# Cosine up products in one-pass pieces from the fourth chunk on, and a planner that orders from both ends

## The chip, the cores and the metric

The kernel runs on one core of a Trainium2 chip. The metric is the device time of one execution in microseconds (us). Engines are named as in the profile: PE (TensorE; PEld is its weight load), DVE (VectorE), ACT (ScalarE), POOL (GpSimd) and SP, which issues the transfers.

## The reference

A Fourier mixing of the input along the sequence and the feature axis, of which the real part is kept, then a two-layer network with a leaky ReLU between:

```python
# x: 8 x 3008 x 256, w_in: 256 x 2048, w_out: 2048 x 256, all float32
X = np.fft.fft(x, axis=1)
X = np.fft.fft(X, axis=2)
x = X.real.astype(np.float32).reshape(8 * 3008, 256)
h = x @ w_in
g = np.maximum(0.01 * h, h)
out = (g @ w_out).astype(np.float32)
```

## The kernel before, in words

**The mathematics.** The transform over features is folded into `w_in` once, at the start: `wf(0, ...)` holds the weights of the cosine part and `wf(1, ...)` those of the sine part, 128 rows by 2048 hidden columns each. The transform over the sequence (`even_rows`, `odd_rows`, `butterfly`) makes `mix_sb[0]` and `mix_sb[1]`, the cosine and sine parts of one batch element with the frequencies as columns, in units: 16 units, two for a batch element. A column of frequency k and the one of -k have the same cosine and opposite sine products, so a hidden value is cosine + sine for the one and cosine - sine for the other. One feature row that doesn't fit in 128 (the Nyquist row, `nb_sb`, with its weights `wn`) is put into the cosine bank beforehand by ScalarE: that is the *seed*.

**Chunks and steps.** The columns are cut into 23 chunks of 504 or 498 columns (`Chunk`, index `t` from 0); a batch element has three, the first only two because its first columns go through a start-up path (`HEAD`, `START`). Each chunk has 16 steps, one for each block of 128 hidden values (`f`). A step (`up`, `up_end`, `hidden`):

- ACT writes the seed into a cosine bank in PSUM (`seed`), two banks in turn for each of cosine and sine;
- PE adds the cosine product, weights `wf(0)` by `mix_sb[0]`, to the seed, and makes the sine product in a sine bank;
- ACT copies the cosine bank to SBUF, DVE writes copy + sine and copy - sine as hidden blocks (`block_sb`), ACT applies the leaky ReLU to them.

The second layer (`sum`, `product`, `combine`) multiplies the hidden blocks with `w_out` in a scheme with fewer products than the plain one: DVE and POOL form sums of blocks (`SUMS`), PE multiplies them with stored combinations of weights (26 products of four matmuls for a chunk, 104 down products, each 252 or 249 columns), and ACT and DVE combine the results (`part_sb`) and send them out. Their weights are loaded anew for every chunk into a ring of eight places (`wr`), six ahead.

**Exact parts.** A float32 matmul is done as two records on PE, a matmul whose operands are of type float32r as one. From chunk 2 on (`PARTED_FROM = 2`) the sine product is done in three float32r matmuls. Each operand is split: `high` is the value scaled by 1 - 2^-13 and rounded to float32r, `low` is what is left, and `both` combines the two. The three products high x high, low x low, both x both are summed in the bank, and between the second and the third ACT scales the bank by 1 + 1/4096. The third is issued in `up_end`. The pieces of the sine columns are made in `parts`, once for a chunk: ACT writes `high`, DVE `both`, POOL `low`, into one of two `mixed` tiles in turn (`mixed[t % 2]`). The pieces of the weights are made once, in `parted_weights`, stored in DRAM (`parted_dram`) and loaded step by step, 192 KB each, four steps ahead, into the four places where the sine weights `wf(1)` lay (`Parted`).

**The order.** After the head, nothing is issued in the order of the code. `rest` calls the helpers in the order of an event list (steps, with offsets such as `UP_FROM`, `UP_END`, `PARTS_AT`), and each call to an engine is only recorded (`Order`, `Taker`). That order fixes what depends on what: reads, writes, buffers reused. `Order.hand_on` then derives the dependences (`connect`), plays the program through with a price for each instruction (`Op.cost`, `SEEN`, and `PORT_LEFT` for instructions of DVE and POOL that may not overlap), and emits all instructions sorted by the start that this gives (`time`). When an engine is free, `time` takes the ready instruction with the earliest `latest`, a due time found by going back from PE's instructions in the order of the code. Since all are emitted from one line, every profile row reads L481.

Of the kernel before, what the change touches and what calls it, by code (L numbers as in the profile page):

```python
# [19 lines left out]
P = 128  # L20
# [121 lines left out]
PARTED_FROM = 2  # L142
UPPER, SHIFT = 1.0 - 2.0**-13, 2.0**12
PARTS_AT, PARTED_WEIGHTS_AT, UP_END = -2.7, 18, 0.2
# [193 lines left out]
SEEN = {"PE": 0.053, "ACT": 0.033, "DVE": 0.033, "POOL": 0.078, "SP": 0.05}  # L338
NAMES = {"tensor": "PE", "scalar": "ACT", "vector": "DVE", "gpsimd": "POOL", "sync": "SP"}
# [124 lines left out]
class Order:  # L464
# [11 lines left out]
    def hand_on(self):  # L476
        self.connect()
        self.time()
        for op in sorted(self.ops, key=lambda op: (op.start, op.at)):
            how = {name: viewed(a) for name, a in op.how.items()}  # L480
            op.made = getattr(op.real, op.method)(*map(viewed, op.args), **how)  # L481
            if op.gate is not None:
                self.add_gate(op.made, op.gate.made)

    def connect(self):
        places = {}
        for at, op in enumerate(self.ops):
            op.at = at
            op.busy, op.took, op.port = op.cost()
            to = op.args[0] if op.args else op.how["out"]  # L490
            reads = [a for a in (*op.args[1:], *op.how.values()) if is_ap(a)]
            name, written = stretches_of(to)
            for a in reads:
# [18 lines left out]
            op.before.discard(at)  # L512
            for b in op.before:
                self.ops[b].after.append(at)

    def time(self):
        ops, engines = self.ops, ("PE", "ACT", "DVE", "POOL", "SP")
        t = 0.0
# [6 lines left out]
        for op in reversed(ops):  # L525
            for b in op.after:
                op.latest = min(op.latest, ops[b].latest - SEEN[ops[b].engine] - op.took)
# [102 lines left out]
def tile_fnet_leaky_relu(  # L630
# [32 lines left out]
    small_sb = const.tile([P, NF + 10], F32, name="small")  # L663
    half_sb = const.tile([P, 568 + 2 * KC + 384], F32, name="half")
# [231 lines left out]
    wf_cos = const.tile([P, F], F32, name="wf_cos")  # L896
    wf_sin = [late.tile([P, WN], F32, name=f"wf_sin{i}", tag=f"wf{i}") for i in range(F // WN)]

    def wf(i, at, n):

        if i == 0:
            return wf_cos[:, at : at + n]
        return wf_sin[at // WN][:, at % WN : at % WN + n]
# [5 lines left out]
    parted_dram = dram.tile([NF, P, 3 * P], F32, name="parted_dram")  # L909
# [5 lines left out]
    angle, inf, lrelu, touched = (small_sb[:, NF + at : NF + at + n] for at, n in ((0, 6), (6, 2), (8, 1), (9, 1)))  # L915
# [205 lines left out]
    def parted_weights(f):  # L1121


# [3 lines left out]
        here = mixed[f // 2 % 2][:, 0 : 6 * P].rearrange("p (f i n) -> p f i n", f=2, i=3)  # L1127
        src = wf(1, f * P, 2 * P).rearrange("p (f n) -> p f n", f=2)
# [5 lines left out]
        nc.sync.dma_start(parted_dram[f : f + 2].rearrange("f p n -> p f n"), here.bitcast(F32).rearrange("p f i n -> p f (i n)"))  # L1134

    class Parted:


        def __init__(self):
            self.places, self.count = [], NF * (len(chunk) - PARTED_FROM)  # L1140

        def load(self, i):
            n = F // WN
            if i >= self.count:
                return
            if i < n:
                self.places.append(Late(wf_sin[i][:, 0 : 3 * P], F32R, lambda: late.tile([P, 3 * P], F32R, name=f"parted{i}", tag=f"wf{i}")))
            nc.sync.dma_start(self.places[i % n].bitcast(F32), parted_dram[i % NF])

        def weight(self, i, part):  # L1150
            return self.places[i % (F // WN)][:, part * P : (part + 1) * P]
# [421 lines left out]
    class Chunk:  # L1573
# [27 lines left out]
        def parts(self):  # L1601
# [10 lines left out]
        def product_of_parts(self, bank, at, i, start=False):  # L1612
            m = mixed[self.t % 2].rearrange("p (i n) -> p i n", i=3)
            nc.tensor.matmul(bank[:, 0 : self.w], lhsT=parted.weight(at, i), rhs=m[:, i, 0 : self.w],
                             start=start, stop=True, skip_group_check=True)

        def seed(self, f):
            nc.scalar.activation(cos_ps[self.half(f)][:, 0 : self.w], nb_sb[:, self.lo : self.lo + self.w], ACT.Copy, scale=wn[:, f : f + 1])

        def up(self, f):  # L1620
            cos, sin = cos_ps[self.half(f)], sin_ps[self.half(f)]
            in_parts = self.t >= PARTED_FROM
            if in_parts:
                at = NF * (self.t - PARTED_FROM) + f
                self.product_of_parts(sin, at, 0, start=True)
                self.product_of_parts(sin, at, 1)
                nc.scalar.activation(sin[:, 0 : self.w], sin[:, 0 : self.w], ACT.Copy, scale=1.0 + 1.0 / SHIFT)
            for i, bank in enumerate((cos, sin)[: 2 - in_parts]):
                nc.tensor.matmul(bank[:, 0 : self.w], lhsT=wf(i, f * P, P), rhs=mix_sb[i][:, self.lo : self.lo + self.w],
                                 start=(i == 1), stop=True, skip_group_check=True)  # L1630
            if not in_parts and self.t == PARTED_FROM - 1 and f % (WN // P) == WN // P - 1:
                parted.load(f // (WN // P))
# [6 lines left out]

        def up_end(self, f):  # L1640
            at = NF * (self.t - PARTED_FROM) + f
            self.product_of_parts(sin_ps[self.half(f)], at, 2)
            parted.load(at + F // WN)
# [175 lines left out]
    def rest():  # L1819
# [3 lines left out]
        parted = Parted()  # L1823
        every.extend(Chunk(t) for t in range(count))
        events = []
        for t in range(count):
            for f in range(NF):
                events.append((16 * t + UP_FROM + f, 3, t, f))
                events.append((16 * t + UP_FROM + f + (UP_END if t >= PARTED_FROM else 0.0), 5, t, f))
# [4 lines left out]
            if t >= PARTED_FROM:  # L1834
                events.append((16 * t + PARTS_AT, 4, t, 0))
# [51 lines left out]
        for _, kind, t, i in events:  # L1887
            if kind == 0:
                start_work(16 * t + i)
                if 0 <= 16 * t + i - PARTED_WEIGHTS_AT < NF // 2:  # L1890
                    parted_weights(2 * (16 * t + i - PARTED_WEIGHTS_AT))
# [18 lines left out]
            elif kind == 4:  # L1910
                every[t].parts()
            elif kind == 3:
# [3 lines left out]
                part = every[t]  # L1916
                made = part.up(i)
# [7 lines left out]
                waiting.clear()  # L1925
            else:
                part = every[t]
                if t >= PARTED_FROM:
                    part.up_end(i)
                waiting[:] = [part.hidden(*made)]  # L1930
# [247 lines left out]
```

## Time and profile before

| | |
|---|---|
| median of 3 runs | 1783.54 us (1782.3 to 1785.22) |
| profiled execution | 1785.57 us, its span 1783.8 us |
| PE, PEld busy | 1760.2, 1396.4 us |
| DVE, ACT, POOL busy | 1560.5, 1250.0, 1084.1 us |
| mean granted TensorE clock | 0.997 |
| moved by DMA | 315.26 MB, 177 GB/s on the mean |

The span is the time from the first to the last instruction in the profiled execution. Busy time is that in which an engine has at least one instruction under way; PEld overlaps PE. A row such as `sin_psa<-mixed,parted` names what is written and what is read: `cos_ps` and `sin_ps` are the banks of the up products, `sum_ps` those of the down products, `dft_ps` that of the transform, each with a letter for the bank; `mixed` holds the pieces of the columns, `parted` those of the weights, `wr` the down weights, `part` the results under combination, `block` the hidden values.

### The profile page before, as it was taken

The numbers are of one execution on the slowest core, as the hardware profiler recorded it, in microseconds if no ns is written. First come the engines' busy times: TensorE is split into PE (matmuls) and PEld (weight loads), VectorE is DVE, ScalarE is ACT, GpSimd is POOL, SyncE is SP. The second block draws the span as 40 slices with busy tenths as digits, with TensorE's granted clock in tenths as the row PEclk, the third lists the DMA queues.
The fourth block names the chain that finished last, engine by engine and source line by source line (L and its number), as shares of the span: only waits on it lengthen the run. The fifth ranks groups of instructions, "written<-read, shape, count | busy, mean of one in ns | idle before, by whom it ended". The sixth has DMA issues, their size and how long they took to land.

```text
span 1783.8 us, 24565 instructions
## 1 busy us (share of the span) xinstructions
PE 1760.2 (99%) x7568; PEld 1396.4 (78%) x7568; DVE 1560.5 (87%) x2635; ACT 1250.0 (70%) x2230; POOL 1084.1 (61%) x480
## 2 busy tenths in 40 slices
PE   9999999999999999999999999999999999999999
PEld 7867687778877888777887778877787777887788
DVE  8897888998899998898998988898989997877887
ACT  4687567876777767777677767777677786767750
POOL 2247476666766665766657657676575765576630
PEclk9999999999999999999999999999999999999999
DMA  7573456655556556555566545755557555555454
GB/s 257 165 253 137 128 159 213 202 164 172 184 182 201 157 172 207 176 187 164 169 221 190 167 148 166 245 172 165 149 172 232 170 158 153 170 150 161 146 145 140
DMA packets 194690, 315.26 MB, mean 177 GB/s; under 512 B 22896, under 2 KB 104432, under 8 KB 194560
## 3 DMA queue, kind: packets, MB, share of 16 engines
q1 hardware_dynamic: 194416, 313.69, 56.8%
q8 instruction: 61, 1.00, 0.2%
q14 instruction: 69, 0.57, 0.1%
q10 hardware_dynamic: 144, 0.00, 0.0%
HBM read 278.92 MB, written 34.68 MB: 176 GB/s over the span
## 4 chain that ended last, share of the span: by engine, by line
PE 88%; DVE 6%; DMA 2%; ACT 2%; issue 1%; SPq 0%; DVEq 0%; ACTq 0%
PE sum_psc L481 20%; PE sum_psa L481 17%; PE sum_psb L481 16%; PE cos_psb L481 8%; PE cos_psa L481 8%; PE sin_psb L481 7%; PE sin_psa L481 7%; PE dft_ps L481 3%; DVE block L481 3%; DVE xt L481 2%; DVE part L481 2%; ACT block L481 1%; DMA out_dram<-part 1%; DMA xt<-in_x_dram 1%; ACT part L481 0%
## 5 line engine op out<-in xcount | busy, mean ns | idle before, releaser
L481 POOL TENSOR_TENSOR block<-block 128x1008 f32<-128x1008 f32 (+2 forms) x402 | 1008.8, 2520 | 535.0 <-DVE block L481 298.0
L481 ACT ACTIVATE block<-block 128x504 f32<-128x504 f32 (+3 forms) x611 | 439.3, 733 | 238.2 <-DVE block L481 232.8
L481 PE MATMUL sum_psc<-block,wr 128*128 128x252 f32 (+1 forms) x1896 | 487.0, 376 | 0.0
L481 PEld LDWEIGHTS sum_psc<-block,wr 128*128 128x128 f32 x1896 | 358.5, 190 | 102.4 <-issue 64.5
L481 PE MATMUL sum_psb<-block,wr 128*128 128x252 f32 (+1 forms) x1536 | 399.5, 376 | 0.3 <-DVE part L481 0.3
L481 PE MATMUL sum_psa<-block,wr 128*128 128x252 f32 (+1 forms) x1544 | 396.9, 377 | 0.6 <-DVE wr L481 0.5
L481 DVE TENSOR_TENSOR block<-block 128x1008 f32<-128x1008 f32 (+2 forms) x249 | 362.3, 1463 | 0.3
L481 PEld LDWEIGHTS sum_psa<-block,wr 128*128 128x128 f32 x1544 | 293.0, 191 | 86.2 <-issue 54.3
L481 PEld LDWEIGHTS sum_psb<-block,wr 128*128 128x128 f32 x1536 | 286.7, 190 | 81.8 <-issue 51.8
L481 DVE TENSOR_TENSOR block<-cos,sin_psa 128x504 f32<-128x504 f32 (+1 forms) x356 | 224.8, 670 | 98.6 <-PE sin_psa L481 81.9
L481 DVE TENSOR_TENSOR block<-cos,sin_psb 128x504 f32<-128x504 f32 (+1 forms) x380 | 239.2, 670 | 47.7 <-PE sin_psb L481 42.6
L481 PE MATMUL sin_psb<-mixed,parted 128*128 128x504 f32 (+1 forms) x504 | 242.5, 524 | 13.1 <-ACT sin_psb L481 13.0
L481 DVE TENSOR_TENSOR part<-part 128x252 f32<-128x252 f32 (+1 forms) x342 | 231.3, 698 | 0.9 <-ACT part L481 0.5
L481 PE MATMUL sin_psa<-mixed,parted 128*128 128x504 f32 (+1 forms) x504 | 230.5, 511 | 0.7 <-ACT sin_psa L481 0.5
L481 PE MATMUL cos_psb<-mixc,wf_cos 128*128 128x504 f32 (+1 forms) x380 | 190.9, 584 | 0.0
L481 PE MATMUL cos_psa<-mixc,wf_cos 128*128 128x504 f32 (+2 forms) x372 | 183.1, 574 | 0.0
L481 DVE TENSOR_TENSOR xt<-xt 128x512 f32<-128x512 f32 (+5 forms) x225 | 152.7, 697 | 1.4 <-DMA xt<-in_x_dram 1.1
L481 ACT ACTIVATE cos_psb<-nb,small 128x504 f32<-128x504 f32 (+1 forms) x190 | 129.6, 682 | 4.9
L481 ACT COPY cos<-cos_psa 128x504 f32<-128x504 f32 (+1 forms) x178 | 102.6, 577 | 37.5 <-PE cos_psa L481 36.4
L481 ACT COPY cos<-cos_psb 128x504 f32<-128x504 f32 (+1 forms) x190 | 109.2, 575 | 27.6 <-PE cos_psb L481 26.0
L481 ACT ACTIVATE cos_psa<-nb,small 128x504 f32<-128x504 f32 (+2 forms) x180 | 122.4, 680 | 4.8
L481 ACT ACTIVATE sin_psa<-sin_psa 128x504 f32<-128x504 f32 (+1 forms) x168 | 96.2, 572 | 36.2 <-PE sin_psa L481 35.2
(162 smaller groups left out, 1520.5 us busy)
## 6 DMA issues: line engine op xcount, KB each, us to landing
wr<-w_dram SPq DMA_DIRECT2D x575, 256.0 KB, 2.8
parted<-parted_dram SPq DMA_DIRECT2D x336, 192.0 KB, 2.6
xt<-in_x_dram SPq DMA_DIRECT2D x28, 1024.0 KB, 6.5
out_dram<-part SPq DMA_DIRECT2D x120, 126.0 KB, 2.3
out_dram<-part SPq DMA_DIRECT2D x64, 124.5 KB, 2.2
tabe<-in_seq_tab_dram SPq DMA_DIRECT2D x29, 190.0 KB, 2.8
w_dram<-block SPq DMA_DIRECT2D x18, 256.0 KB, 4.2
block<-in_w_in_dram SPq DMA_DIRECT2D x8, 512.0 KB, 4.1
```

What stands on the lines that cost most here:

```text
L481: op.made = getattr(op.real, op.method)(*map(viewed, op.args), **how)
```

## The change

1. The cosine product is done in three float32r products too, from chunk 3 on (`PARTED_FROM = (3, 2)` for cosine and sine). Its first two are added to the seed, ACT scales the cosine bank by 1 + 1/4096 in between, and the third is added after that. So that the seed isn't scaled, it is made with `wn_less`, the Nyquist weights divided by that factor. In the list of events the two third products, and with them the copy of the cosine bank, the next seed and `hidden`, come in `up_end`, half a step later (`UP_END = 0.5`).
2. The pieces of the cosine columns are made by the same three instructions, once for a chunk. Sine and cosine have one `mixed` tile each now (`mixed[1 - part]`), not two in turn; the events that make them stand at 0.8 and 0.9 of a step into the chunk, where sine's stood at 2.7 steps ahead of it.
3. The pieces of the cosine weights are made in steps 32 to 47, one block a step, stored in `parted_dram`, and loaded like those of the sine. `wf_cos` becomes four tiles that give their places to these pieces.
4. The planner plays the program through up to 30 times (`ROUNDS`). After each round it goes through the program from the end with the starts just found (`time_back`), takes the due times from that, and plays it forward again; the shortest of the 30 orders is used. A result that PE takes from another engine counts as ready half a microsecond later than before (`SLACK = 0.5`).
5. Smaller: the angle table moves to another tile, and `parted_weights` no longer waits for a gate before its first subtraction.

The diff, cut to its core:

```diff
-PARTED_FROM = 2
+PARTED_FROM = (3, 2)
+UP_PER = 1.0
-PARTS_AT, PARTED_WEIGHTS_AT, UP_END = -2.7, 18, 0.2
+PARTS_AT, PARTED_WEIGHTS_AT, UP_END = (0.9,0.8), (32, 18), 0.5
...
+SLACK = 0.5
+ROUNDS = 30
...
     def hand_on(self):
         self.connect()
-        self.time()
+        self.place()
...
+        best = None
+        for i in range(ROUNDS):
+            if i:
+                self.time_back()
+            self.time()
+            total = max(op.start + op.took for op in ops)
+            if best is None or total < best[0]:
+                best = total, [op.start for op in ops]
+        for op, start in zip(ops, best[1]):
+            op.start = start
+
+    def time_back(self):
...
+            while soon[e] and soon[e][0][0] <= t + 1e-9:
+                k = heapq.heappop(soon[e])[1]
+                heapq.heappush(now[e], (-ops[k].start - ops[k].took, k))
...
+        for op in ops:
+            op.latest = -placed[op.at]
...
-                    ready[b] = max(ready[b], t + (SEEN[to.engine] if what == "done" else 0.0))
+                    ready[b] = max(ready[b], t + (to.seen + (SLACK if b >= self.first and to.engine == "PE" else 0.0) if what == "done" else 0.0))
...
-    wf_cos = const.tile([P, F], F32, name="wf_cos")
-    wf_sin = [late.tile([P, WN], F32, name=f"wf_sin{i}", tag=f"wf{i}") for i in range(F // WN)]
+    wfs = [[late.tile([P, WN], F32, name=f"wf_{part}{i}", tag=f"wf_{part}{i}") for i in range(F // WN)] for part in ("cos", "sin")]
...
-    def parted_weights(f):
+    def parted_weights(part, f):
...
+            nc.scalar.activation(wn_less, wn, ACT.Copy, scale=1.0 / (1.0 + 1.0 / SHIFT))
+        n = 1 + part
+        to = mixed[f // 2 % 2][:, 0 : 6 * P] if part else mixed[1][:, f % 3 * 3 * P : (f % 3 + 1) * 3 * P]
...
-        wait_for_gate(nc.gpsimd.tensor_tensor(both, src, high, op=ALU.subtract))
+        nc.gpsimd.tensor_tensor(both, src, high, op=ALU.subtract)
...
-            m = mixed[self.t % 2].rearrange("p (i n) -> p i n", i=3)
-            high, low, both = (m[:, i, 0 : self.w] for i in range(3))
-            src = mix_sb[1][:, self.lo : self.lo + self.w]
+            high, low, both = self.pieces(part)
+            src = mix_sb[part][:, self.lo : self.lo + self.w]
             nc.scalar.activation(high, src, ACT.Copy, scale=UPPER)
             nc.vector.scalar_tensor_tensor(both, in0=high, scalar=1.0 + 1.0 / SHIFT, in1=src, op0=ALU.mult, op1=ALU.subtract)
             nc.gpsimd.tensor_tensor(low, src, high, op=ALU.subtract)
...
+        def pieces(self, part):
+            m = mixed[1 - part].rearrange("p (i n) -> p i n", i=3)
+            return [m[:, i, 0 : self.w] for i in range(3)]
...
         def up(self, f):
...
+            for part, bank in reversed(list(enumerate(self.banks(f)))):
+                if self.in_parts(part):
+                    self.product_of_parts(bank, part, f, 0, start=(part == 1))
+                    self.product_of_parts(bank, part, f, 1)
+                    nc.scalar.activation(bank[:, 0 : self.w], bank[:, 0 : self.w], ACT.Copy, scale=1.0 + 1.0 / SHIFT)
+                else:
+                    nc.tensor.matmul(bank[:, 0 : self.w], lhsT=wf(part, f * P, P), rhs=mix_sb[part][:, self.lo : self.lo + self.w],
+                                     start=(part == 1), stop=True, skip_group_check=True)
...
+        def up_end(self, f):
+            cos, sin = self.banks(f)
+            for part, bank in enumerate((cos, sin)):
+                if self.in_parts(part):
+                    self.product_of_parts(bank, part, f, 2)
+                    parted[part].load(NF * (self.t - PARTED_FROM[part]) + f + F // WN)
```

More of the change, by code (lines that the diff above doesn't have):

```diff
@@ L485, in connect @@
     def connect(self):
-        places = {}
+        places, made = {}, set()
         for at, op in enumerate(self.ops):
@@ L492, in connect @@
             name, written = stretches_of(to)
+            if isinstance(to, Late) and name not in made:
+                made.add(name)
+                written = [(0, to.ap[0][0])]
             for a in reads:
@@ L512, in connect, with place @@
             op.before.discard(at)
+            op.seen = SEEN[op.engine]
             for b in op.before:
                 self.ops[b].after.append(at)
-    def time(self):
-        ops, engines = self.ops, ("PE", "ACT", "DVE", "POOL", "SP")
-        t = 0.0
+    def place(self):
+        ops, t = self.ops, 0.0
         for op in ops:
@@ new lines, in place, with at @@
+        for op, start in zip(ops, best[1]):
+            op.start = start
+    def time_back(self):
+        ops, engines = self.ops, ("PE", "ACT", "DVE", "POOL", "SP")
+        left, placed, opens = [len(op.after) for op in ops], [0.0] * len(ops), [0.0] * len(ops)
+        free, port = dict.fromkeys(engines, 0.0), {"DVE": 0.0, "POOL": 0.0}
+        soon, now, events, count = {e: [] for e in engines}, {e: [] for e in engines}, [], 0
+        def at(t, e):
+            nonlocal count
+            count += 1
+            heapq.heappush(events, (t, count, e))
+        for op in ops:
+            if not op.after:
+                heapq.heappush(soon[op.engine], (0.0, op.at))
+        for e in engines:
+            at(0.0, e)
+        while events:
+            t, _, e = heapq.heappop(events)
+            if t < free[e] - 1e-9:
+                continue
+            while soon[e] and soon[e][0][0] <= t + 1e-9:
+                k = heapq.heappop(soon[e])[1]
+                heapq.heappush(now[e], (-ops[k].start - ops[k].took, k))
+            k, waits, other = None, [], port["POOL" if e == "DVE" else "DVE"]
+            while now[e] and k is None:
+                first = heapq.heappop(now[e])
+                if ops[first[1]].port and other > t + 1e-9:
+                    waits.append(first)
+                else:
+                    k = first[1]
+            for first in waits:
+                heapq.heappush(now[e], first)
+            if k is None:
+                if waits:
+                    at(other, e)
+                elif soon[e]:
+                    at(soon[e][0][0], e)
+                continue
+            op = ops[k]
+            placed[k] = free[e] = max(t + op.busy, opens[k])
+            if op.port:
+                port[e] = placed[k]
+            for b in op.before:
+                to = ops[b]
+                opens[b] = max(opens[b], placed[k] + (to.busy if to.engine == e == "PE" else to.took + op.seen))
+                left[b] -= 1
+                if not left[b]:
+                    when = max(0.0, opens[b] - to.busy)
+                    heapq.heappush(soon[to.engine], (when, b))
+                    at(max(when, free[to.engine]), to.engine)
+            at(free[e], e)
+        for op in ops:
+            op.latest = -placed[op.at]
@@ L528, in time @@
+    def time(self):
+        ops, engines = self.ops, ("PE", "ACT", "DVE", "POOL", "SP")
         left, ready = [len(op.before) for op in ops], [0.0] * len(ops)
@@ L1146, in load, with weight @@
             if i < n:
[L1147 to L1151, printed above, removed]
+                of = ("cos", "sin")[self.part]
+                self.places.append(Late(wfs[self.part][i][:, 0 : 3 * P], F32R,
+                                        lambda: late.tile([P, 3 * P], F32R, name=f"parted_{of}{i}", tag=f"wf_{of}{i}")))
+            nc.sync.dma_start(self.places[i % n].bitcast(F32), parted_dram[self.part, i % NF])
+        def weight(self, i, piece):
+            return self.places[i % (F // WN)][:, piece * P : (piece + 1) * P]
     reach = [w % 4 for w in range(8)]
@@ L1610, in parts, with product_of_parts @@
             nc.gpsimd.tensor_tensor(low, src, high, op=ALU.subtract)
-        def product_of_parts(self, bank, at, i, start=False):
-            m = mixed[self.t % 2].rearrange("p (i n) -> p i n", i=3)
-            nc.tensor.matmul(bank[:, 0 : self.w], lhsT=parted.weight(at, i), rhs=m[:, i, 0 : self.w],
+        def pieces(self, part):
+            m = mixed[1 - part].rearrange("p (i n) -> p i n", i=3)
+            return [m[:, i, 0 : self.w] for i in range(3)]
+        def product_of_parts(self, bank, part, f, i, start=False):
+            nc.tensor.matmul(bank[:, 0 : self.w], lhsT=parted[part].weight(NF * (self.t - PARTED_FROM[part]) + f, i), rhs=self.pieces(part)[i],
@@ L1620, in up, with banks @@
+        def banks(self, f):
+            return cos_ps[self.half(f)], sin_ps[self.half(f)]
         def up(self, f):
[L1621 to L1632, printed above, removed]
+            for part, bank in reversed(list(enumerate(self.banks(f)))):
[3 more added lines that the diff above has]
+                    nc.scalar.activation(bank[:, 0 : self.w], bank[:, 0 : self.w], ACT.Copy, scale=1.0 + 1.0 / SHIFT)
+                else:
+                    nc.tensor.matmul(bank[:, 0 : self.w], lhsT=wf(part, f * P, P), rhs=mix_sb[part][:, self.lo : self.lo + self.w],
+                                     start=(part == 1), stop=True, skip_group_check=True)
@@ L1633, in up @@
+            for part in (1, 0):
+                if self.t == PARTED_FROM[part] - 1 and f % (WN // P) == WN // P - 1:
+                    parted[part].load(f // (WN // P))
+        def up_end(self, f):
[4 more added lines that the diff above has]
+                    parted[part].load(NF * (self.t - PARTED_FROM[part]) + f + F // WN)
             k, g = divmod(f, 4)
@@ L1822, in rest @@
         count = len(chunk)
-        parted = Parted()
+        parted = [Parted(part) for part in range(2)]
         every.extend(Chunk(t) for t in range(count))
@@ L1833, in rest @@
                 events.append((16 * t + (DOWN_FROM + m / PER_STEP if t else FIRST_DOWN + m / FIRST_PER), 2, t, m))
-            if t >= PARTED_FROM:
-                events.append((16 * t + PARTS_AT, 4, t, 0))
+            for part in range(2):
+                if t >= PARTED_FROM[part]:
+                    events.append((16 * t + PARTS_AT[part], 4, t, part))
         for r in range(16 * count + 18):
@@ L1889, in rest @@
                 start_work(16 * t + i)
-                if 0 <= 16 * t + i - PARTED_WEIGHTS_AT < NF // 2:
-                    parted_weights(2 * (16 * t + i - PARTED_WEIGHTS_AT))
+                for part in range(2):
+                    f = (16 * t + i - PARTED_WEIGHTS_AT[part]) * (1 + part)
+                    if 0 <= f < NF:
+                        parted_weights(part, f)
                 now[0] = START_SHARES.get(i, 0.0) if 16 * t + i < 17 else SHARES[0] if 16 * t + i < 32 else SHARES[1]
@@ L1910, in rest @@
             elif kind == 4:
-                every[t].parts()
+                every[t].parts(i)
             elif kind == 3:
@@ L1915, in rest @@
                     assert 2 * b + (hi > UW[1]) <= transformed[-1], (t, transformed, len(folds.queue))
-                part = every[t]
-                made = part.up(i)
+                every[t].up(i)
+                for to in sum(waiting, []):
+                    nc.scalar.activation(to, to, ACT.Lrelu)
+                waiting.clear()
+            else:
+                made = every[t].up_end(i)
                 seed_next(16 * t + i)
@@ L1924, in rest @@
                 behind[:] = [None]
[L1925 to L1930, printed above, removed]
+                waiting[:] = [every[t].hidden(*made)]
                 some(0)
```

41 lines of the change are left out of this document (20 added, 21 removed).

## The prediction

> **What bounds the kernel now.** I read the page's busy shares first, then PE's own waits, then the engines in six equal stretches of the steady part, then PE in order of time, then the groups by form. The shares, with two rows of the table of waits that has PE as the waiting engine:
>
> ```profile
> span 1783.8 us, 24565 instructions
> PE 1760.2 (99%) x7568; PEld 1396.4 (78%) x7568; DVE 1560.5 (87%) x2635; ACT 1250.0 (70%) x2230; POOL 1084.1 (61%) x480
> PE 88%; DVE 6%; DMA 2%; ACT 2%; issue 1%; SPq 0%; DVEq 0%; ACTq 0%
> PE sin_psb L481 <- ACT sin_psb L481: 13.0, 9, 2.8
> PE sin_psa L481 <- ACT sin_psa L481: 0.5, 1, 0.5
> ```
>
> PE is busy all the time and holds 88% of the chain that ended last. Its one repeated wait is that of a sine product for ScalarE's scaling of the same bank: 13.5 us in 10 waits. The stretches show how near the others are (columns: stretch, its length, then busy time and instructions of PE, PEld, DVE, ACT, POOL, clock, DMA share, GB/s):
>
> ```profile
> 300.00:532.00 232.00, 231.59 (x1006) 185.06 (x1005) 206.91 (x342) 171.39 (x303) 157.94 (x66) 1.00 0.59 181
> 764.00:996.00 232.00, 232.00 (x1011) 186.10 (x1010) 213.26 (x360) 175.48 (x313) 148.66 (x61) 1.00 0.60 186
> 996.00:1228.00 232.00, 230.02 (x993) 183.52 (x992) 204.17 (x354) 175.55 (x334) 153.34 (x61) 0.99 0.58 179
> sum 1392.00, PE 1378.19 PEld 1100.45 DVE 1228.15 ACT 1021.89 POOL 916.16; mean PE 229.70 PEld 183.41 DVE 204.69 ACT 170.32 POOL 152.69
> ```
>
> DVE is busy 88% on the mean (204.69 of 232) and 92% in the fullest stretch, where PE never stops. So PE sets the time and DVE is close behind it.
>
> Busy records of PE overlap, so prices come from starts, in PE's order of time in one step:
>
> ```profile
> 942.62 1.00 PE L481 MATMUL sum_psc<-block,wr 128*128 128x249 f32 x4
> 943.28 0.80 PE L481 MATMUL sin_psa<-mixed,parted 128*128 128x504 f32 x2
> 943.92 1.01 PE L481 MATMUL cos_psa<-mixc,wf_cos 128*128 128x504 f32 x2
> 944.76 1.00 PE L481 MATMUL sum_psc<-block,wr 128*128 128x249 f32 x4
> 945.42 0.58 PE L481 MATMUL sin_psa<-mixed,parted 128*128 128x504 f32 x1
> 945.83 1.42 PE L481 MATMUL sum_psc<-block,wr 128*128 128x249 f32 x6
> ```
>
> The full cosine product (two records) lasts from 943.92 to 944.76: 0.84 us. Four records of the down product take the same, 0.84 (0.21 each), so the group from 942.62 ends at 943.46, and the two sine pieces fill 943.46 to 943.92: 0.23 each. (A one-pass record begins early, when its weights are in; the next plain one marks its end.) The third: 944.76 + 0.84 = 945.60, to 945.83, 0.23 again.
>
> The groups that price the rest, and the span of one group by the tile's view (durations min/median/max, first and last start):
>
> ```profile
> L481 POOL TENSOR_TENSOR block<-block 128x1008 f32<-128x1008 f32 x270 | 681.8, 2536 | 372.5 <-DVE block L481 211.4 <-PE sum_psb L481 60.2 <-PE sum_psa L481 58.8
> L481 ACT ACTIVATE sin_psa<-sin_psa 128x504 f32<-128x504 f32 x112 | 64.3, 574 | 18.5 <-PE sin_psa L481 17.6
> L481 DVE TENSOR_TENSOR part<-part 128x252 f32<-128x252 f32 x225 | 146.2, 668 | 0.8 <-ACT part L481 0.5
> L481 DVE TENSOR_TENSOR part<-part,sum_psc 128x252 f32<-128x252 f32 x90 | 34.9, 410 | 6.4 <-PE sum_psc L481 4.9 <-ACT part L481 1.4
> L481 DVE SCALAR_TENSOR_TENSOR mixed<-mixed,mixs 128x504 fp32r<-128x504 f32 x14 | 13.2, 944 | 0.0
> L481 PE MATMUL sin_psa<-mixed,parted x504: 383/573/583, 225.9 to 1727.4; 128*128 128x504 f32 x112, 128*128 128x498 f32 x56
> L481 PEld LDWEIGHTS sin_psa<-mixed,parted x504: 186/190/198, 225.9 to 1727.4; 128*128 128x128 f32 x168
> L481 ACT ACTIVATE mixed<-mixs x21: 599/617/628, 217.5 to 1593.3; 128x504 fp32r<-128x504 f32 x14, 128x498 fp32r<-128x498 f32 x7
> L481 POOL TENSOR_TENSOR mixed<-mixs,mixed x21: 1247/1293/2220, 218.2 to 1606.0; 128x504 fp32r<-128x504 f32 x14, 128x498 fp32r<-128x498 f32 x7
> L481 DVE SCALAR_TENSOR_TENSOR mixed<-mixed,mixs x21: 664/672/2771, 221.3 to 1629.6; 128x504 fp32r<-128x504 f32 x14, 128x498 fp32r<-128x498 f32 x7
> L481 ACT ACTIVATE mixed<-wf_sin x8: 400/406/430, 89.0 to 184.5; 128x256 fp32r<-128x256 f32 x8
> L481 POOL TENSOR_TENSOR mixed<-wf_sin,mixed x8: 721/732/1756, 89.8 to 185.0; 128x256 fp32r<-128x256 f32 x8
> ```
>
> Sine in pieces runs over 21 chunks of 16 steps on two banks: 504 records a bank, three a step. From step 0 of its first chunk to step 14 of its last (20.9 chunks) there are 1501.5 us: a chunk takes 72 us.
>
> **The change part by part.** Times are set against the profiled execution (span 1783.8, with what lies around it 1785.6); the median of the runs is 1783.5, 2.1 lower.
>
> *Cosine products.* One full product becomes three one-pass ones from the fourth chunk on: 20 chunks of 16 steps, 320 times. Each saves 0.84 - 3 x 0.23 = 0.15; with the 0.23 rounded up (0.46 for a pair, and 0.22 to 0.23 alone) 0.155. That is **-50 us**, all on PE's path. Three weight loads in place of two add 320 x 0.19 = 61 us to PEld; each lies under the product before it (0.19 under 0.23), so nothing; uncovered it would cost 0.19 each.
>
> *The scaling in the cosine bank.* It is one more ScalarE instruction a step, 0.574 us, and the third product waits for it; on PE's queue the down products stand behind that product, and on ScalarE's the copy of the cosine, the next seed and the leaky ReLUs stand behind the scaling. VectorE waits for the copy. The row for that wait is sine's: 10 waits, 13.5 us, 1.35 each in 336 steps. Doubled as it is, +13; with the planner's new slack of 0.5 us on everything PE takes from another engine, at best all of sine's go too, -13.5. Between: 656 steps give 20 waits, each 0.5 shorter, 17 us, which is **+3**; I take this, because the row is of the same wait and the slack is a third of its mean.
>
> *Pieces at the start of a chunk.* Sine's pieces had two buffers in turn, now sine has one and cosine the other. A chunk's pieces can be written only when the last step before has read them: 0.62 on ScalarE, then on GpSimd 1.29 for sine and 1.29 for cosine, some 3.2 us before all products of the new chunk may run. Cover: the down products of earlier chunks, 104 a chunk at 0.42 = 44 us, which need no pieces. Bounds 0 and 20 x 3.2 = 64. GpSimd stood idle in a third of the steady part (152.69 of 232), and PE has the cover at hand in every row of the step above: **0**, and the rest to the rivals.
>
> *The load on the others.* ScalarE: 1250 + 320 x 0.574 + 20 x 0.62 + 32 x at most 0.41 for the weights' pieces = 1459, 84% of 1742. In a steady chunk it is 52.9 (73.4% of 72) + 9.2 + 0.6 = 62.7 of 69.5, 90%; its fullest stretch before had 175.55 of 232, 76%. That it keeps up at 90% no row shows; what it would cost is PE's wait for the scaling, so it stands there, with the +13 as its upper end. GpSimd: 20 x 1.29 + 32 x about 0.73 = +49 of its idle 700. VectorE: 63.5 a chunk (88.2% of 72) and 0.67 (0.94 where GpSimd blocks it) for the cosine's piece: 64.2 to 64.5, in a chunk of 72 - 16 x 0.155 = 69.5 this is 92.4 to 92.8%. The fullest stretch with an unbroken PE had 91.9%; at that share the chunk takes 64.2/0.919 = 69.8, 0.3 more, **+6** in 20 chunks. Lower end 0 (a better order blocks VectorE less); upper end the mean share, 88.2%, which is the slower rival.
>
> *Transfers.* 320 more loads of pieces on SP and 16 stores:
>
> ```profile
> q1 hardware_dynamic: 194416, 313.69, 56.8%
> wr<-w_dram SPq DMA_DIRECT2D x575, 256.0 KB, 2.8
> parted<-parted_dram SPq DMA_DIRECT2D x336, 192.0 KB, 2.6
> GB/s 257 165 253 137 128 159 213 202 164 172 184 182 201 157 172 207 176 187 164 169 221 190 167 148 166 245 172 165 149 172 232 170 158 153 170 150 161 146 145 140
> ```
>
> They add 66 MB: 380 in 1742 us is 218 GB/s and 56.8 x 380/314 x 1784/1742 = 70% of the engines' time; slices of 245 to 257 GB/s are in the page. A piece is asked for four steps (17 us) before it is read and lands in 2.6; the SP queue waits for the third product before each, and the down weights queued behind have six of eight places loaded ahead. **0**; without that lead each late piece would cost PE its 2.6.
>
> *The planner.* Thirty rounds, forward and back, and the shortest order kept; the first round is the present method with the slack added. All that PE can still win is what it waits for: 0 to the 13.5 counted above. The head, the first three chunks' products and the tail have no other work.
>
> Sum: 1785.6 - 50 + 3 + 0 + 6 + 0 = 1744.6; less the 2.1 by which the profiled execution lies over the median: **1742 us**, 2.3% faster.
>
> **The rivals.** *The new order also takes PE's waits away.* The 13.5 vanish and VectorE keeps up: 1785.6 - 50 - 13.5 - 2.1 = 1720. For it: those waits are few and long (up to 2.8), the kind that better foresight removes. Against: every engine is fuller.
>
> *Chunk starts are not covered.* Each start costs PE 1 us of the 3.2 (a third of it, as long as one down group of the rows above): 1742 + 20 = 1762; with all 3.2, 1806. For it: both pieces now go through GpSimd one behind the other, whose usual instruction lasts 2.54 us. Against: 44 us of other products a chunk.
>
> *VectorE and GpSimd take over, slower than before.* Where two of VectorE's inputs lie in SBUF it waits out GpSimd's instruction: 668 ns for the sum with both inputs in SBUF against 410 for the one fed from PSUM. More GpSimd work in a shorter chunk means more such waits. If VectorE can't be used over its mean share, a chunk takes 64.5/0.882 = 73.1, 1.1 more than now: 1783.5 + 22 = 1806. It decides where the reachable share falls under 64.5/72 = 89.6%. Against: the stretch at 91.9%. The Trainium skill, page "SBUF — State Buffer", section "SBUF: two separate sides", has the pair of ports as a lock held for the whole instruction, where the loser fully blocks; by that rule, the 668 against 410 agree.
>
> *The time on PE is not what counts: no change.* The saved time comes back elsewhere, 1783. Against: PE waits for nothing in 232 us of the fullest stretch, and its products follow each other at 0.21 and 0.23. The Trainium skill, page "Perfetto Trace Analysis", section "Identifying the Most-Contended Engine", calls matmul busy time a poor measure and takes the weight loads' share instead, 78% here; by that rule PE would have room, but the loads are short (0.19) under products of 0.21 to 0.42 that leave no gap, so the trace speaks against it.
>
> **How the numbers follow.** Forecast 0.61 (its own range 1730 to 1756: waits +13, VectorE 92.8% at 91.9, against none of either), the waits gone 0.16, chunk starts 0.12, no change 0.04, slower 0.07. The range runs from 1720 to 1772, the second for starts of 1.5 us each. A measurement of this kernel can tell about 0.2% (the three runs span 0.16%): faster 0.61 + 0.16 + 0.11 = 0.88, same 0.04, slower 0.08 with the worst of the chunk starts.
>
> **What would show it.** Right: 960 records of cosine pieces on the two cosine banks (3 x 320), PE still at 98% or more, a pair of cosine pieces 0.46 apart from its neighbours, ScalarE near 1460, VectorE at 90 to 93%. Wrong: PE waits over 40 us; VectorE's share over 94% with PE idle; PE waits for GpSimd or ScalarE pieces once in a chunk; waits for transfers of pieces; a granted clock under 0.997 in the stretches.

## The result and the profile after

The changed kernel takes 1759.51 us (median; 1756.13 to 1786.64 in 4 runs) against 1783.18 us for the kernel before (median of 4): a ratio of 0.9859, interval 0.984 to 0.9879, 1.4% faster. The one run at 1786.64 had a granted clock of 0.949 and is left out of the ratio (the median of the other three is 1758.58). The forecast was 1742 us, range 1720 to 1772.

The page of the changed kernel (all rows now read L484), and its transfers:

```profile
span 1758.7 us, 26452 instructions
PE 1721.2 (98%) x7888; PEld 1450.5 (82%) x7888; DVE 1596.4 (91%) x2655; ACT 1362.4 (77%) x2595; POOL 1124.6 (64%) x532
PE 65%; DVE 22%; ACT 5%; DMA 4%; issue 2%; POOL 1%; SPq 0%; DVEq 0%; POOLq 0%; ACTq 0%
q1 hardware_dynamic: 242800, 379.77, 68.7%
```

PE is still busy nearly all the time, but its share of the chain that ended last fell from 88% to 65%, and VectorE's rose from 6% to 22%. The products themselves became as short as forecast; PE in order of time:

```profile
963.43 0.57 PE L484 MATMUL cos_psb<-mixed,parted_cos 128*128 128x504 f32 x1
963.84 0.63 PE L484 MATMUL cos_psa<-mixed,parted_cos 128*128 128x504 f32 x2
964.30 0.62 PE L484 MATMUL sin_psa<-mixed,parted_sin 128*128 128x504 f32 x2
964.76 1.44 PE L484 MATMUL sum_psa<-block,wr 128*128 128x252 f32 x6
```

From 963.84 to 964.30 and on to 964.76 there are two pairs of pieces, 0.46 each. So the 50 us were saved, and the span fell by 25.1 (1783.8 to 1758.7): half of the saving came back as time in which PE waits. By busy time PE's idle part went from 23.6 to 37.5 us. The other 11 us don't show in the busy column. They fit the weight loads, which wait on the same queue: their waits for VectorE come to some 40 us (12 before), those for ScalarE to 28 (25 before), and the record of a one-pass product, which begins with its weight load, can cover such a wait. What PE waits for has changed. The table of waits, PE's rows, then those of its weight loads:

```profile
PE sin_psb L484 <- DVE block L484: 6.2, 7, 1.4
PE sum_psb L484 <- DVE part L484: 5.9, 6, 2.5
PE cos_psb L484 <- ACT cos_psb L484: 5.3, 7, 1.3
PE sin_psa L484 <- DVE block L484: 4.2, 6, 1.3
PE sum_psa L484 <- DVE part L484: 3.2, 3, 1.7
PE cos_psa L484 <- ACT cos_psa L484: 2.9, 5, 1.2
PEld sin_psb L484 <- DVE block L484: 14.9, 29, 1.8
PEld cos_psb L484 <- ACT cos_psb L484: 10.9, 17, 1.6
PEld sum_psb L484 <- DVE part L484: 8.7, 9, 2.9
```

Before, PE waited for ScalarE's scaling of the sine bank. Now most of its waits (some 21 of 33 us) are for VectorE, which has not yet read a sine bank (`block`) or a bank of down products (`part`) that PE wants to write. The stretches of the steady part, summed, with the row that answers to the fullest one of before:

```profile
764.00:996.00 232.00, 226.06 (x1059) 193.68 (x1057) 216.06 (x345) 191.98 (x365) 155.70 (x65) 1.00 0.72 227
sum 1392.00, PE 1361.64 PEld 1170.71 DVE 1269.85 ACT 1142.11 POOL 946.83; mean PE 226.94 PEld 195.12 DVE 211.64 ACT 190.35 POOL 157.80
```

VectorE is at 91% on the mean (88% before), GpSimd at 68% (66%). In the stretch where PE never stopped before, VectorE now has 216.06 us (213.26) and PE 226.06 (232.00). How one such stall comes about can be followed in order of time (all engines; rows of the others left out):

```profile
1006.99 2.34 POOL L484 TENSOR_TENSOR block<-block 128x1008 f32<-128x1008 f32 x1
...
1007.07 2.80 DVE L484 TENSOR_TENSOR xt<-xt 128x512 f32<-128x512 f32 x1
...
1009.80 1.25 DVE L484 TENSOR_TENSOR block<-cos,sin_psb 128x504 f32<-128x504 f32 x2
...
1010.50 0.62 ACT L484 ACTIVATE block<-block 128x504 f32<-128x504 f32 x1 [1.95 <-DVE block L484]
...
1011.11 0.72 PE L484 MATMUL sin_psb<-mixed,parted_sin 128*128 128x498 f32 x2 [1.05 <-DVE block L484]
```

GpSimd starts a sum at 1006.99. VectorE, 0.08 us later, starts an instruction with both inputs in SBUF, whose like from PSUM takes 0.67; it lasts 2.80 us and ends 0.54 after GpSimd's (1009.33). Only then does VectorE read the sine bank. ScalarE has waited 1.95 us for that, and PE 1.05 us for the bank to be free. Not each wait of PE has such an instruction just before it: of its 26 waits for VectorE, 18 have one in the 3 us before.

### The profile page after: what moved, and what is told of

It reads as the page before. It is cut to its first block, busy times and chain, and to the rows that moved or that the text cites. A ratio compares the mean times of both kernels' runs of the same rounds, so it can differ in the third digit from the quotient of the medians.

```text
span 1758.7 us, 26452 instructions
## 1 busy us (share of the span) xinstructions
PE 1721.2 (98%) x7888; PEld 1450.5 (82%) x7888; DVE 1596.4 (91%) x2655; ACT 1362.4 (77%) x2595; POOL 1124.6 (64%) x532
## 3 DMA queue, kind: packets, MB, share of 16 engines
q1 hardware_dynamic: 242800, 379.77, 68.7%
## 4 chain that ended last, share of the span: by engine, by line
PE 65%; DVE 22%; ACT 5%; DMA 4%; issue 2%; POOL 1%; SPq 0%; DVEq 0%; POOLq 0%; ACTq 0%
PE sum_psc L484 16%; PE sum_psb L484 13%; PE sum_psa L484 13%; DVE block L484 10%; DVE part L484 6%; PE sin_psb L484 6%; PE cos_psb L484 5%; PE sin_psa L484 5%; PE cos_psa L484 5%; DVE xt L484 3%; DMA out_dram<-part 3%; PE dft_ps L484 2%; ACT block L484 1%; POOL block L484 1%; ACT cos L484 1%
## 5 line engine op out<-in xcount | busy, mean ns | idle before, releaser
L484 POOL TENSOR_TENSOR block<-block 128x1008 f32<-128x1008 f32 (+2 forms) x402 | 1002.1, 2506 | 457.8 <-DVE block L484 294.0
L484 ACT ACTIVATE block<-block 128x504 f32<-128x504 f32 (+3 forms) x603 | 434.0, 739 | 95.7 <-DVE block L484 93.7
L484 PE MATMUL sum_psc<-block,wr 128*128 128x252 f32 (+1 forms) x1896 | 470.2, 375 | 0.8 <-DVE part L484 0.7
L484 PEld LDWEIGHTS sum_psc<-block,wr 128*128 128x128 f32 x1896 | 358.0, 190 | 56.7 <-issue 6.6
L484 PE MATMUL sum_psa<-block,wr 128*128 128x252 f32 (+1 forms) x1544 | 393.7, 375 | 4.2 <-DVE part L484 3.2
L484 PE MATMUL sum_psb<-block,wr 128*128 128x252 f32 (+1 forms) x1536 | 381.8, 377 | 6.2 <-DVE part L484 5.9
L484 PEld LDWEIGHTS sum_psb<-block,wr 128*128 128x128 f32 x1536 | 290.6, 190 | 53.0 <-DVE part L484 8.7
L484 PEld LDWEIGHTS sum_psa<-block,wr 128*128 128x128 f32 x1544 | 290.2, 189 | 50.6 <-issue 9.0
L484 DVE TENSOR_TENSOR block<-block 128x1008 f32<-128x1008 f32 (+2 forms) x249 | 328.2, 1328 | 3.4 <-PE sum_psb L484 2.3
L484 DVE TENSOR_TENSOR block<-cos,sin_psa 128x504 f32<-128x504 f32 (+1 forms) x356 | 225.8, 668 | 45.4 <-ACT cos L484 21.5
L484 DVE TENSOR_TENSOR block<-cos,sin_psb 128x504 f32<-128x504 f32 (+1 forms) x380 | 240.4, 667 | 18.3 <-ACT cos L484 10.7
L484 DVE TENSOR_TENSOR part<-part 128x252 f32<-128x252 f32 (+1 forms) x342 | 238.7, 721 | 0.1
L484 PE MATMUL sin_psb<-mixed,parted_sin 128*128 128x504 f32 (+1 forms) x504 | 220.6, 482 | 6.3 <-DVE block L484 6.0
L484 PE MATMUL sin_psa<-mixed,parted_sin 128*128 128x504 f32 (+1 forms) x504 | 215.4, 473 | 6.2 <-DVE block L484 4.2
L484 PE MATMUL cos_psb<-mixed,parted_cos 128*128 128x504 f32 (+1 forms) x480 | 204.8, 467 | 4.2 <-ACT cos_psb L484 4.2
L484 PE MATMUL cos_psa<-mixed,parted_cos 128*128 128x504 f32 (+1 forms) x480 | 200.0, 461 | 3.4 <-ACT cos_psa L484 2.9
L484 DVE TENSOR_TENSOR xt<-xt 128x512 f32<-128x512 f32 (+5 forms) x225 | 172.5, 781 | 0.2
L484 ACT COPY cos<-cos_psa 128x504 f32<-128x504 f32 (+1 forms) x178 | 103.0, 578 | 54.0 <-PE cos_psa L484 45.5
L484 ACT COPY cos<-cos_psb 128x504 f32<-128x504 f32 (+1 forms) x190 | 109.9, 578 | 36.1 <-PE cos_psb L484 33.2
L484 ACT ACTIVATE cos_psb<-nb,small 128x504 f32<-128x504 f32 (+1 forms) x190 | 129.8, 683 | 2.0
L484 ACT ACTIVATE cos_psa<-nb,small 128x504 f32<-128x504 f32 (+2 forms) x180 | 122.8, 682 | 1.4
L484 PEld LDWEIGHTS sin_psa<-mixed,parted_sin 128*128 128x128 f32 x504 | 94.4, 189 | 26.3 <-DVE block L484 7.7
```

## The experiments

All were timed against the kernel before, with these ratios; the profiles quoted are of the same runs. Each of these kernels is ordered anew by the planner. How much the time scatters from one order to another no run shows, so differences of 8 to 10 us (e11, e12) say less than their intervals do.

| | us (median) | ratio, interval |
|---|---|---|
| the change | 1759.5 | 0.9859, 0.984 to 0.9879 |
| e1 full cosine products, new planner | 1783.2 | 1.0005, 0.9991 to 1.0019 |
| e2 one round, no slack | 1818.4 | 1.0205, 1.0171 to 1.0238 |
| e3 no slack | 1776.6 | 0.9971, 0.9957 to 0.9985 |
| e4 VectorE's sums halved | 1732.0 | 0.9726, 0.9704 to 0.9747 |
| e5 GpSimd's sums halved | 1710.8 | 0.9601, 0.9586 to 0.9615 |
| e6 one round, slack kept | 1820.7 | 1.0215, 1.0189 to 1.024 |
| e7 one sum to VectorE | 1738.3 | 0.975, 0.9734 to 0.9767 |
| e8 three sums to VectorE | 1725.5 | 0.9682, 0.9667 to 0.9696 |
| e9 e1 and three sums to VectorE | 1776.1 | 0.9969, 0.9958 to 0.9979 |
| e10 pieces of the columns made once | 1737.5 | 0.975, 0.9729 to 0.9772 |
| e11 GpSimd's sums in two halves | 1749.9 | 0.9821, 0.9799 to 0.9842 |
| e12 e8 without slack | 1733.2 | 0.9729, 0.9709 to 0.975 |

### Products or order: e1, e2, e6, e3

e1, the order without the products:

```diff
-PARTED_FROM = (3, 2)
+PARTED_FROM = (23, 2)
-PARTS_AT, PARTED_WEIGHTS_AT, UP_END = (0.9,0.8), (32, 18), 0.5
+PARTS_AT, PARTED_WEIGHTS_AT, UP_END = (0.9,0.8), (9999, 18), 0.5
```

> The planner in rounds with its slack, one set of sine pieces and the later end of a step are kept; the cosine products stay full ones. Theory (PE's work is what fell, by 0.155 us in 320 steps; the rounds only make that gain usable): no product is saved, so the time is that of before, 1778 to 1788 us. Rival (the new order brings the gain by itself): 1770 us or less. If the single set of pieces at the chunk starts cost 1 us each, 1800 us or more.

1783.2, ratio 1.0005: no difference. The new order by itself gains nothing.

e2, the products with the old way of ordering:

```diff
-SLACK = 0.5
-ROUNDS = 30
+SLACK = 0.0
+ROUNDS = 1
```

> The cosine products in pieces are kept, the order is found in one forward pass and without slack, as before the change. Theory (the other engines are so full that the old way of ordering can't feed PE): most of the 50 us saved on PE come back as waits, 1780 to 1805 us. Rival (the order hardly matters, the gain is PE's work): 1755 to 1765 us.

1818.4: slower than before by 2%, and worse than the theory asked for. With the old way of ordering the products lose more than they save (the event list is that of the change; whether another list would serve a single pass better wasn't tried). The page of e2:

```profile
span 1814.5 us, 26231 instructions
PE 1758.1 (97%) x7888; PEld 1450.3 (80%) x7888; DVE 1558.2 (86%) x2655; ACT 1394.2 (77%) x2595; POOL 1123.2 (62%) x532
```

No engine is full: 86% on VectorE, less than before. PE idles for 56 us (1814.5 - 1758.1), because in this order the others deliver at the wrong time.

That is 19 us more than in the changed kernel, while the span is 56 longer (1814.5 against 1758.7). Part of the rest is the granted clock. In e2's profiled execution it stands at 0.50 in six stretches, 41 us in all (the mean is 0.989); in the changed kernel in two, 6.8 us in all (0.998). In one of e2's, from 1268.8 to 1279.0, two pairs of sine pieces have records of 1.20 us each, against 0.62 at 964.30 above. Before each of the eight stretches PE had stood idle for about half or more (48 to 77%) of the last 3.4 us. Half of 41 less half of 6.8 is 17 us, an estimate of what the lower clock costs e2 beside the changed kernel. So a long wait of PE is paid for a second time, by slower products after it.

e6, one round with the slack kept (`ROUNDS = 1` alone):

> The changed kernel with one forward pass (its slack of 0.5 kept). Theory (slack and rounds work together: the rounds find the place for PE's products that the slack asks for): without the rounds the slack is just a delay, 1800 us or more, no better than the single pass without slack (1818). Rival (the slack is what makes the gain, the rounds are not needed): 1765 us or less.

1820.7, no better than e2 (the intervals overlap). The slack needs the rounds.

e3, 30 rounds without the slack (`SLACK = 0.0` alone):

> As the changed kernel, but the planner takes no slack for what PE gets from other engines (30 rounds kept). If the slack keeps PE from waits that the plan didn't foresee: PE's waits grow, 1765 to 1775 us. If it only makes a longer plan: 1750 us or less. If it doesn't matter: 1756 to 1763 us.

1776.6: a little slower than the expected stretch. Rounds bring 1818 to 1777, the slack on top of them another 17 us. About half of the 17 is the clock again: its mean is 0.994 in these ten runs and 0.998 in the changed kernel's, and 0.45% of 1777 is 8 us, an estimate.

### What PE waits for: e4, e5, e7, e8

e4 and e5 halve the sums of one engine, with the condition `engine is not None` (VectorE) or `engine is None` (GpSimd):

```diff
-            ins = (engine or nc.gpsimd).tensor_tensor(self.value(16 + i), xa, ya, op=...)
+            to, n = self.value(16 + i), 2 if engine is not None else 4
+            ins = (engine or nc.gpsimd).tensor_tensor(to[:, 0:n], xa[:, 0:n], ya[:, 0:n], op=...)
```

> The sums of hidden blocks that VectorE makes (10 of 28 in a chunk) cover only half of their columns groups, the rest of the sums is left out; everything else is as in the changed kernel, the order found anew. It takes some 0.6 us from each of 249 instructions, about 6 us of VectorE's 66 in a chunk, and as much of the time in which it and GpSimd exclude each other. Theory (PE's new idle time comes from VectorE and GpSimd being full): PE's idle falls back to what it was before the change, 1728 to 1740 us. Rival (chunk starts, ScalarE or transfers hold PE): 1752 to 1760 us.

> The 18 of 28 sums in a chunk that GpSimd makes cover only half of their column groups, the rest is left out; VectorE's work is that of the changed kernel. Theory (VectorE and GpSimd exclude each other, and GpSimd's long sums keep VectorE and the down products waiting): as with VectorE's half sums PE's idle falls back, 1725 to 1740 us, and VectorE's sums with both inputs in SBUF get shorter than 1.28 to 1.36 us. Rival (VectorE's own instructions are the limit, GpSimd isn't): 1750 us or more.

1732.0 and 1710.8. Relief on either engine gives the saving back, so VectorE with GpSimd is what holds PE. e5 leaves VectorE its work and still gains more than e4; it gets under the expected stretch, since PE's waits of before vanish too (it idles 7.7 us, 23.6 before). Its page, and VectorE's sums of down products with both inputs in SBUF, in the changed kernel and in e5 (groups by form):

```profile
span 1709.4 us, 25998 instructions
PE 1701.7 (100%) x7888; PEld 1453.8 (85%) x7888; DVE 1457.3 (85%) x2655; ACT 1386.7 (81%) x2595; POOL 703.0 (41%) x532
```

```profile
L484 DVE TENSOR_TENSOR part<-part 128x252 f32<-128x252 f32 x225 | 151.5, 693 | 0.0
```

```profile
L484 DVE TENSOR_TENSOR part<-part 128x252 f32<-128x252 f32 x225 | 124.6, 570 | 1.5 <-ACT part L484 0.8
```

The same 225 instructions take 693 ns on the mean in the one and 570 in the other, while those that read a sine bank in PSUM (`block<-cos,sin_psb`, 128x504) hardly change, 668 and 674. VectorE's busy time falls by 139 us though it has the same instructions. The single instructions of the changed kernel show why: of the 225, the 149 that begin while GpSimd runs nothing take 0.40 to 0.42 us, the other 76 take 1.25 on the mean and up to 2.59. So a good part of its 91% is time in which GpSimd keeps it out.

If that is so, work should go from GpSimd to the fuller engine. e7 takes 4 out of the list `ON_GPSIMD`, e8 takes out 2, 4 and 14:

```diff
-ON_GPSIMD = (1, 2, 4, 5, 7, 10, 11, 13, 14, 15, 18, 19, 20, 22, 23, 24, 26, 27)
+ON_GPSIMD = (1, 5, 7, 10, 11, 13, 15, 18, 19, 20, 22, 23, 24, 26, 27)
```

> One sum of a chunk (number 4) goes from GpSimd to VectorE, nothing is left out. It takes about 2.3 us a chunk from GpSimd and from the time in which the two exclude each other, and adds 1.19 us to VectorE and to that time. Theory (the exclusion and GpSimd's long instruction are the limit): 1735 to 1752 us. Rival (VectorE's own instruction time is the limit): 23 x 1.19 us more work on the fullest engine, 1765 to 1785 us.

> Sums 2, 4 and 14 go from GpSimd to VectorE where they were on GpSimd, and sum 2 stays or goes likewise (numbers 4 and 14 leave GpSimd; 2 is one of GpSimd's too): three sums moved, nothing left out. Theory of the exclusion: a little better than one sum moved, 1728 to 1748 us. Rival (VectorE's own time): 3 x 23 x 1.19 = 82 us more on VectorE, 1790 us or more.

1738.3 is in the stretch of the exclusion, 1725.5 is 2.5 us under it, better than asked for; both are far from the rival's 1765 and 1790. e8 beats both kernels: it is 3.2% faster than the one before and 1.8% faster than the changed one (0.9682 against 0.9859). Its page and the sum of its stretches:

```profile
span 1724.1 us, 26239 instructions
PE 1706.8 (99%) x7888; PEld 1451.5 (84%) x7888; DVE 1596.0 (93%) x2721; ACT 1371.5 (80%) x2595; POOL 989.0 (57%) x466
sum 1392.00, PE 1381.65 PEld 1201.14 DVE 1298.09 ACT 1164.68 POOL 822.81; mean PE 230.27 PEld 200.19 DVE 216.35 ACT 194.11 POOL 137.13
```

VectorE is at 93% (216.35 of 232), fuller than in the changed kernel, and PE idles less (1.73 us of 232 against 5.06). GpSimd's 135.6 us less (1124.6 - 989.0) is the difference. If each VectorE instruction is set against the shortest tenth of its own form, what they run over comes to 265 us in the changed kernel, 231 before, 111 in e5 and 192 in e8, an estimate of the time in which VectorE is kept out.

### Whether that limit came with the change: e9

e1 and the three sums moved:

> The full cosine products (as in e1) together with the three sums moved from GpSimd to VectorE (as in e8). Theory (the moved sums pay only because the shorter products made VectorE and GpSimd the limit): before the change PE alone set the time, so the moved sums bring little, 1775 to 1785 us. Rival (the three sums were too much for GpSimd before as well): 1740 us or less, as much better than e1 as e8 is than the changed kernel (34 us).

1776.1: the moved sums bring 0.4% (0.9969 against 1.0005) where PE has its full products, and 1.8% (0.9682 against 0.9859) with the short ones. So VectorE and GpSimd became the limit with the change.

Read the other way, the four runs price the products. With GpSimd as full as it was, they bring 23.7 us (e1 to the change, 1783.2 to 1759.5); with three sums moved, 50.6 (e9 to e8, 1776.1 to 1725.5; the mean clock of 0.999 against 1.0 has some 2 us in that). That is the 50 us by which the products are shorter.

### Chunk starts, long instructions, slack: e10, e11, e12

e10 makes the pieces of the columns once:

```diff
-                if t >= PARTED_FROM[part]:
+                if t == PARTED_FROM[part]:
                     events.append((16 * t + PARTS_AT[part], 4, t, part))
```

> The pieces of the columns are made for the first chunk of each part only and read by all later chunks; their making in the later chunks is left out (ScalarE 1.2, VectorE 1.3, GpSimd 2.7 us a chunk). Nothing waits at the start of a chunk any more. If the single set of pieces costs PE 1 us at each start or more, beside the load: 1715 to 1730 us. If it is the load alone, it should be like the one sum moved (2.3 us of GpSimd's time a chunk), 1733 to 1745 us. If chunk starts and this load are both covered: 1755 us or more.

1737.5, what the expectation gave for the load alone: 2.7 us of GpSimd less in a chunk, with 1.2 of ScalarE and 1.3 of VectorE, gain as much as the 2.3 of e7, where VectorE got 1.19 more. That fits starts that cost PE nothing by themselves; the run takes away wait and load together, so it isn't shown apart.

e11 splits each of GpSimd's sums into two instructions:

```diff
+            to, n = self.value(16 + i), 4 if engine is not None else 2
+            for at in range(0, 4, n):
+                ins = (engine or nc.gpsimd).tensor_tensor(to[:, at : at + n], xa[:, at : at + n], ya[:, at : at + n], op=...)
```

> Each of GpSimd's 18 sums of a chunk is done in two instructions of half its columns, nothing left out. The time in which GpSimd holds VectorE off is the same or a little more, but no single wait is longer than about 1.3 us. Theory (the total of the time in which the two exclude each other counts): no gain, 1755 to 1775 us. Rival (the length of one GpSimd instruction, 2.3 us that can't be broken off, is what stalls VectorE): 1750 us or less.

1749.9, on the rival's bound: some 9 us better, and the two intervals just overlap (0.984 to 0.9842). GpSimd's busy time rises to 1278.2 us (1124.6 in the changed kernel) and it is still no slower. That speaks for the length of one instruction counting as well as the total, but the margin is too small to show it; moving one sum gains twice as much.

e12 is e8 with `SLACK = 0.0`:

> As e8 (three sums moved), the planner without its slack. If the slack covers what the chip does otherwise than planned, whichever engine is full: worse by some 10 to 20 us, 1735 to 1745 us, as in e3. If it only helped because VectorE and GpSimd were overfull: 1722 to 1728 us.

1733.2, 8 us worse than e8, between the two expectations. Here the clock hardly plays a part (a mean of 0.9995 against 1.0, 1 us). Without the clock the slack is worth some 9 us in e3 and 7 here, so that it depends on how full GpSimd is isn't shown. Which waits it avoids here these runs don't show: the rows of PE's waits hardly differ.

## Why the prediction was right, and where its sum was off

The direction and the range held; the sum came out 17 us low (1742 against 1759.5). It missed the forecast's own range, 1730 to 1756, by 3.5 us. The time lies inside the full range only in the part that was kept for uncovered chunk starts, and those are not what cost it, so that the range held is in part luck. By its steps:

- **The products, -50.** Right: a pair of pieces takes 0.46, 960 records of cosine pieces are there, and e9 to e8 bring 50.6. (A one-pass record begins with its own weight load and not when the weights are in, in the row at 943.28 at 943.25; the price doesn't hang on that.)
- **The scaling, +3.** Too high: PE's three rows of waits for ScalarE's scaling come to 9.1 us (5.3 and 2.9 above, and 0.9 for sine), against 13.5 before; the sum had 17. The step is off by some 7 us, in the good direction, and hides as much of the next one's miss.
- **VectorE's load, +6.** This is the term that was mis-sized, by 13 us or more. It took the share of the fullest stretch, 91.9%, as what VectorE can reach, and so asked for 0.3 us a chunk. A busy share of VectorE can't be read that way: it holds the time in which GpSimd keeps it out, and that falls as GpSimd has less to do: by the estimate above 265 us in the changed kernel, 192 in e8, 111 in e5, with GpSimd busy for 1124.6, 989.0 and 703.0 us. In e8 VectorE reaches 93.3% and PE hardly waits; in e2 it stands at 86% and PE idles 56 us. PE's own rows of waits for VectorE alone are 19.5 us in the changed kernel (6.2, 5.9, 4.2 and 3.2 above), where the table before had 0.3 for `part` and none for `block`. With the weight loads' waits (40 us, 12 before) this is where most of the saving went.
- **GpSimd's +49 us "of its idle 700", priced at nothing.** Wrong for the same reason. GpSimd's instructions are not hidden by its idle time while VectorE has to wait for them: e7 shows 21 us for 2.3 us of GpSimd a chunk, and e10 22 us for 2.7 with some work of the other two.
- **Chunk starts, 0.** Nothing speaks against it: PE's table has one wait for pieces, of 0.2 us (`DVE mixed`), and e10 gives what the load alone would. But the work of the pieces is not free.
- **Transfers, 0.** Right: 379.77 MB on the queue and 68.7% against 380 and 70%; the median landing of pieces went from 2.6 to 3.3 us, and PE's table has no wait for one.
- **ScalarE, 1459 us.** Too high, 1362: 365 more instructions, 320 of them of 0.57 us, add 206 us of durations but only 112 of busy time, since the records of instructions that follow each other overlap.
- **The planner, 0 to 13.5.** Undervalued. It could gain only what PE waited for on the old work, and e1 shows just that: nothing. On the new work it is the difference between 1818 and 1759, a part of it by the clock, for which the prediction has no term.
- **The rivals.** The slower one named the right place, VectorE and GpSimd shutting each other out, but it asked for the whole saving and 22 us more, where half the saving was lost. The Trainium skill, page "SBUF — State Buffer", section "SBUF: two separate sides", has the loser block for the whole instruction; the 2.80 us at 1007.07, which end 0.54 after GpSimd's instruction, agree. With the old order that rival's sign would have come true (e2), though through the order and not through a full VectorE. "The time on PE is not what counts" fell with e5 and e8, where PE is at 99 to 100% and the time at its lowest. The Trainium skill, page "Perfetto Trace Analysis", section "Identifying the Most-Contended Engine", judges TensorE by the weight loads' share, beside the share of peak arithmetic, and not by its busy time. That share is 85% in e5, where PE idles 7.7 of 1709.4 us, so the trace does not show the room that it would suggest.
- **The signs.** ScalarE near 1460 did not come (1362). Of the signs of being wrong, PE's waits stayed under 40 us by busy time (37.5); with the 11 us that the busy column doesn't show they are over it. The granted clock was under 0.997 in one stretch, 0.99 from 532 to 764.

## What to carry to other kernels

When a change shortens the engine that sets the time, price the next engine by what it must do plus what it waits for inside its instructions, not by its busy share: compare the same instruction where it begins while GpSimd runs nothing and where GpSimd is at work (0.41 and 1.25 us here). Where VectorE and GpSimd shut each other out, a sum can cost less on VectorE (1.2 us here) than on GpSimd (2.3), even with VectorE at 91%. And when the order is planned, test new work and new order apart: here each alone gave nothing or a loss, and both together 1.4%. Look at the granted clock, too, when waits grow.

## What was not expected of the hardware

VectorE at 93% beside PE at 99% (e8) was faster than VectorE at 91% with more on GpSimd (the changed kernel). Moving 66 sums took 135.6 us off GpSimd and cost VectorE no busy time at all (1596.4 and 1596.0): the 79 us that they add to VectorE (66 x 1.2) it saves in being kept out (265 to 192 us by the estimate above).
